# B and C casts behind bank copies, a spread decode, two tiles of the second layer by turns, and a shorter sign step

## The chip, the cores and the metric

The kernel runs on one core of a Trainium2 chip. The metric is the device time of one execution in microseconds (us). Times of a whole run stand beside a profiled execution, whose instructions the hardware profiler recorded. The engines are called as in the profile: PE (TensorE matmul; PEld its weight loads), DVE (VectorE), ACT (ScalarE), POOL (GpSimd) and SP (SyncE, which here only issues DMAs). An L and a number is a line of the kernel before.

## The reference

A chunked scan with decay, then two feed-forward layers on its output (batch 4, 8 heads, 768 positions, head size 32, state size 16). Cut to what is computed:

```python
for c in range(nc):                     # the reference goes by chunks of 32
    cum = np.cumsum(log_a[chunk]); L = np.exp(cum[i] - cum[j]) * causal
    y_intra = ((C @ B.T) * L) @ x       # per batch and head
    y_inter = (C @ state) * np.exp(cum)
    state = np.exp(sum(log_a)) * state + B.T @ (x * decay_from_j)
x = y.transpose(...).reshape(3072, 256)                       # tokens x (heads * head size)
h = max(max(x @ w1, x @ w2), x @ w3);  x = h @ w_out          # layer 1: 256 -> 768 -> 256
gate = 1 / (1 + exp(-(x @ w_gate)));  val = x @ w_val
return (gate * val) @ w_out2                                  # layer 2: 256 -> 1536 -> 256
```

The weights come in as 64-bit floats, seen as pairs of 32-bit words; the rest is float32.

## The kernel before

**Scan.** The kernel takes chunks of 96 positions, so there are 8 chunks and, with four of the 32 batch-head units at a time, 64 attention steps k = 8c + g. Step k does four matmuls s (B against C, L270 for the first 16 steps, L273 after), multiplies them with the decay (L285 on DVE, or L281 on ACT with L282 on POOL), and does four matmuls y (L291). For the steps from 16 on, s reads B and C as three bfloat16 parts each, stacked over partitions in `bi` and `cs`. `split_bc(c)` makes them for one chunk: it loads B and C into `bc` (L234); then three times over ACT casts what is left into `parts` (L239), SP sends `parts` to its places in `bi` and `cs` (L244, six, four and two DMAs for the three parts), and POOL takes the part away from `bc` (L248). `bc` and `parts` have one buffer, `bi` and `cs` two. The decay rows `dec` are loaded with L206 and scanned on DVE (L228). `prepare(k)` calls all of this ahead of its use; it adds `split_bc(c + 1)` to the pipe at step 8c.

**Layers.** Both layers go over six tiles of 512 tokens. A unit is a tile t and a block m of 128 hidden columns: layer 1 has 6 units a tile and three products (18 matmuls u, then 6 matmuls o into the accumulators), layer 2 has 12 units a tile and two products (12 u, 6 o). All of these are L338 to L340: each product is a sum of three, with operands split in a high and a low word. The three PSUM banks for u go round. A bank is emptied by `most` (layer 1: ACT copies the first bank, L383; DVE takes the maxima, L385 and L387) or `gated` (layer 2: ACT sigmoid, L392; DVE product, L394). Then ACT makes the high word (`hi`, L376), and POOL or DVE the low word (`lo`, L378). The matmuls o of a unit (`down`) come one unit later. The two accumulator banks `o0`, `o1` are copied out at the end of a tile (L357 to y1 for layer 1, L363 for layer 2). `split_y(t)` makes high and low words of layer 2's input (L369, L371).

**Decode.** Each weight piece of 128 x 512 (layer 1: 12 pieces `a`; layer 2: 24 pieces `b`, every other one 128 x 256) is loaded raw (L127) and turned into two float32 words: three ACT instructions (L136 the sign, into the upper half-words of the zeroed tiles `sg`; L138 the exponent, in place; L139 the low word, rounded), two on DVE (L142 shift and OR with the sign, L144 integer add), one on ACT (L148) and one on POOL (L150).

**Order.** The program is emitted as coroutines: `tick` moves each active one a stage on, and a slot (24 to a tile of layer 1) is one product or one `down`. `slot_end` starts attention steps so that a tile's input is there in time: for the first two tiles one at a time, from the third in pairs. `weights_tick` starts one decode a slot. The order on each engine is then laid by the framework's planner, which simulates the program with its own costs and may place an instruction well ahead of those that were emitted before it. Each engine then works through its list in that order. `tc.issue_after(x)` binds what is traced inside it to stand behind x on x's engine.

```python
act.copy(parts[:, p], r)                                   # L239
act.activation(out=sg...[..., 1], in_=f1.bitcast(F32), func=AF.Identity, scale=2.0 ** -112)   # L136
dve.scalar_tensor_tensor(out=t, in0=f1, scalar=3, in1=sg, op0=ALU.logical_shift_left, op1=ALU.bitwise_or)   # L142
```

Of the kernel before, what the change touches and what calls it, by code (L numbers as in the profile page):

```python
# [12 lines left out]
U32 = mybir.dt.uint32  # L13
AF = mybir.ActivationFunctionType
# [52 lines left out]
def scan_attention_then_ffn(ctx: ExitStack, tc: tile.TileContext, xh, ah, bch, pick, bn, w1, w2, w3,  # L67
# [48 lines left out]
    sgs = [stp.tile([128, DEC // 128, 128], I32, tag=f"sg{k}", bufs=1, name=f"sg{k}") for k in range(2)]  # L116
    blocks_done = []
    for sg in sgs:
        pool.memset(sg, 0)

# [9 lines left out]
    def decode(raw, wpool, blocks, name):  # L130
        nb = raw.shape[1]
        f1 = raw[..., 1]
        r = stp.tile([128, DEC // 128, 128], I32, tag="r", bufs=3, name=f"r_{name}")[:, 0:nb]
        sg = sgs[len(blocks_done) % len(sgs)][:, 0:nb]
        blocks_done.append(name)
        act.activation(out=sg.bitcast(F16).rearrange("p b (n t) -> p b n t", t=2)[..., 1], in_=f1.bitcast(F32),  # L136
                       func=AF.Identity, scale=2.0 ** -112)
        act.mul(f1.bitcast(F32), f1.bitcast(F32), 2.0 ** -112)  # L138
        act.mul(r, raw[..., 0].bitcast(U32), 2.0 ** -29)  # L139
        yield  # L140
        t = stp.tile([128, DEC // 128, 128], I32, tag="t", bufs=2, name=f"t_{name}")[:, 0:nb]
        dve.scalar_tensor_tensor(out=t, in0=f1, scalar=3, in1=sg, op0=ALU.logical_shift_left,  # L142
                                 op1=ALU.bitwise_or)
        dve.tensor_tensor(out=r, in0=t, in1=r, op=ALU.add)  # L144
# [3 lines left out]
        act.copy(w[:, 0], r.bitcast(F32))  # L148
# [4 lines left out]
    def weights_tick():  # L153
        if loaded:
            pipe.add(decode(*loaded.pop(0)))
# [75 lines left out]
    def split_bc(c):  # L231
# [6 lines left out]
        for p in range(3):  # L238
            act.copy(parts[:, p], r)  # L239
# [7 lines left out]
            if p < 2:  # L247
                pool.tensor_tensor(out=r, in0=r, in1=parts[:, p], op=ALU.subtract)  # L248
                yield

    steps = [(c, g) for c in range(NC) for g in range(NG)]
    done = [0]
    last = [None]
# [57 lines left out]
    def prepare(k):  # L311

        c, g = divmod(k, NG)
        if g == 0 and 0 < c < NC - 1:
            load_x(c + 1)
            pipe.add(split_bc(c + 1))
# [27 lines left out]
    def down(t, m, mn, w, hl, finish):  # L344
        if m == 0:
            acc[0] = [pso.tile([128, TT], F32, tag=f"o{d}", name=f"o{mn}_{t}_{d}")
                      for d in range(KD)]
        first = len(w) - KD
        for d in range(KD):
            three(acc[0][d], [m], mn, w, lambda k: first + d, lambda k: hl[0], lambda k: hl[1])  # L350
        if m == mn - 1:
            pipe.add(finish(t, acc[0]))
# [27 lines left out]
    def most(s, banks, hl):  # L380

        yield
        act.copy(s, banks[0])  # L383
# [3 lines left out]
        dve.tensor_tensor(out=s, in0=banks[2], in1=s, op=ALU.max)  # L387
        yield from hidden(s, hl, pool)

    def gated(s, banks, hl, eng):  # L390
        yield
        act.activation(out=s, in_=banks[0], func=AF.Sigmoid)  # L392
        yield
        dve.tensor_tensor(out=s, in0=banks[1], in1=s, op=ALU.mult)  # L394
# [169 lines left out]
```

## Time and profile before

| | |
|---|---|
| three timed runs | 606.14, 601.85, 602.65 us; median 602.65 us |
| the profiled execution: its time | 604.28 us |
| the profiled execution: span from first to last instruction | 602.5 us |
| mean granted TensorE clock over the span | 0.974 |
| PE busy | 563.0 us (93%) |
| DVE, ACT, POOL busy | 317.5, 260.0, 186.0 us |

Busy time is the time in which an engine has an instruction at work, added over the span. The clock is a share of full speed (2.4 GHz): 1.00 is full, 0.50 the lower level of 1.2 GHz. What an idle stretch is worth is read from the wait that ends it.

### The profile page before, as it was taken

How to read it: one execution, taken by the hardware profiler on the slowest of the kernel's cores; microseconds unless marked ns; L12 is line 12 of the kernel's file. 1: busy time of each engine (PE TensorE's matmuls, PEld its weight loads, DVE VectorE, ACT ScalarE, POOL GpSimd, SP SyncE). 2: the span in 40 equal slices, each digit the busy share in tenths (PEclk: the TensorE clock that was granted, in tenths of full speed). 3: DMA queues.
4: the chain of work that ended last, by engine and by line, in shares of the span. 5: the costliest groups of instructions: out<-in, count | busy, mean ns of one | idle time of the engine just before them, and what ended most of it. 6: DMA issues, size and time to landing. Idle time of an engine off the chain costs nothing.

```text
span 602.5 us, 8006 instructions
## 1 busy us (share of the span) xinstructions
PE 563.0 (93%) x2992; PEld 444.7 (74%) x2992; DVE 317.5 (53%) x467; ACT 260.0 (43%) x475; POOL 186.0 (31%) x207
## 2 busy tenths in 40 slices
PE   5778797997989999999999999999999999999997
PEld 4656575675767777777768888888888888888885
DVE  4899962644745755368987133344344334334332
ACT  5777653224233223279897243233233223223322
POOL 3668874335453424237668210000000000000000
PEclk9859998998999989999999999999999999999999
DMA  7998975373763900099000000000000000000000
GB/s 252 326 313 233 205 183 93 102 132 86 155 134 83 178 28 1 1 316 312 1 2 0 2 35 1 0 1 35 2 0 36 0 1 36 1 1 35 1 0 35
DMA packets 35367, 50.53 MB, mean 84 GB/s; under 512 B 3456, under 2 KB 24320, under 8 KB 35328
## 3 DMA queue, kind: packets, MB, share of 16 engines
q1 hardware_dynamic: 35328, 50.02, 32.0%
q8 instruction: 23, 0.38, 0.3%
q14 instruction: 16, 0.13, 0.1%
HBM read 38.51 MB, written 3.25 MB: 69 GB/s over the span
## 4 chain that ended last, share of the span: by engine, by line
PE 63%; DVE 9%; DMA 8%; ACT 5%; issue 4%; POOL 2%; SPq 1%; DVEq 0%; ACTq 0%; POOLq 0%
PE u L338 14%; PE u L339 14%; PE u L340 14%; PE o L339 7%; PE o L340 6%; PE o L338 6%; DMA cs<-parts 4%; DVE dec L228 2%; DMA dec<-ad 1%; DMA bc<-in_bch 1%; DVE t_b L142 1%; DVE s L387 1%; DVE s L385 1%; PE y L291 1%; POOL lo L378 1%
## 5 line engine op out<-in xcount | busy, mean ns | idle before, releaser
L376 ACT CAST hi<-s 128x512 fp32r<-128x512 f32 x108 | 67.1, 621 | 193.1 <-DVE s L394 153.8
L394 DVE TENSOR_TENSOR s<-u,s 128x512 f32<-128x512 f32 x72 | 49.7, 690 | 126.2 <-PE u L340 125.9
L338 PE MATMUL u<-xt_hi,w_b 128*128 128x512 f32 x288 | 112.4, 390 | 0.8 <-DVE s L385 0.6
L339 PE MATMUL u<-xt_lo,w_b 128*128 128x512 f32 x288 | 112.1, 389 | 0.0
L340 PE MATMUL u<-xt_hi,w_b 128*128 128x512 f32 x288 | 112.1, 389 | 0.0
L338 PE MATMUL u<-xt_hi,w_a 128*128 128x512 f32 x216 | 90.8, 420 | 10.4 <-ACT s L383 5.8
L339 PE MATMUL u<-xt_lo,w_a 128*128 128x512 f32 x216 | 87.2, 404 | 1.8 <-DVE xt_lo L302 1.8
L340 PE MATMUL u<-xt_hi,w_a 128*128 128x512 f32 x216 | 87.0, 403 | 0.0
L378 POOL TENSOR_TENSOR lo<-s,hi 128x512 fp32r<-128x512 f32 x48 | 66.4, 1384 | 64.1 <-ACT hi L376 63.0
L338 PEld LDWEIGHTS u<-xt_hi,w_b 128*128 128x128 f32 x288 | 54.1, 188 | 13.3 <-DVE s L385 1.1
L378 DVE TENSOR_TENSOR lo<-s,hi 128x512 fp32r<-128x512 f32 x60 | 41.5, 692 | 40.6 <-ACT hi L376 40.4
L340 PEld LDWEIGHTS u<-xt_hi,w_b 128*128 128x128 f32 x288 | 54.1, 188 | 11.3
L339 PEld LDWEIGHTS u<-xt_lo,w_b 128*128 128x128 f32 x288 | 54.1, 188 | 11.0
L338 PEld LDWEIGHTS u<-xt_hi,w_a 128*128 128x128 f32 x216 | 42.2, 195 | 25.1 <-ACT s L383 8.0
L228 DVE TENSOR_TENSOR_SCAN dec<-dec,delta 128x388 f32<-128x388 f32 x64 | 57.9, 944 | 3.2 <-DMA dec<-ad 3.0
L339 PE MATMUL o<-lo,w_b 128*128 128x512 f32 x144 | 56.1, 390 | 0.0
L340 PE MATMUL o<-hi,w_b 128*128 128x512 f32 x144 | 56.0, 389 | 0.0
L339 PEld LDWEIGHTS u<-xt_lo,w_a 128*128 128x128 f32 x216 | 42.1, 195 | 10.3 <-DVE xt_lo L302 2.3
L340 PEld LDWEIGHTS u<-xt_hi,w_a 128*128 128x128 f32 x216 | 42.0, 194 | 9.5
L392 ACT ACTIVATE s<-u 128x512 f32<-128x512 f32 x72 | 43.2, 600 | 10.8 <-PE u L340 9.8
L385 DVE TENSOR_TENSOR s<-u,s 128x512 f32<-128x512 f32 x36 | 24.6, 685 | 40.4 <-PE u L340 25.8
L338 PE MATMUL o<-hi,w_b 128*128 128x512 f32 x144 | 45.3, 390 | 0.5 <-ACT hi L376 0.5
(60 smaller groups left out, 761.6 us busy)
## 6 DMA issues: line engine op xcount, KB each, us to landing
dec<-ad SPq DMA_DIRECT2D x30, 388.0 KB, 5.6
raw_a<-in_w SPq DMA_DIRECT2D x18, 256.0 KB, 6.2
bi<-parts SPq DMA_DIRECT2D x36, 128.0 KB, 6.7
cs<-parts SPq DMA_DIRECT2D x36, 96.0 KB, 6.8
xs<-in_xh SPq DMA_DIRECT2D x6, 512.0 KB, 7.1
raw_b<-in_wg SPq DMA_DIRECT2D x12, 256.0 KB, 5.8
raw_b<-in_wv SPq DMA_DIRECT2D x12, 256.0 KB, 5.8
raw_b<-in_wo SPq DMA_DIRECT2D x12, 256.0 KB, 5.8
```

The source lines that it names most:

```text
L142: dve.scalar_tensor_tensor(out=t, in0=f1, scalar=3, in1=sg, op0=ALU.logical_shift_left, op1=ALU.bitwise_or)
L228: dve.tensor_tensor_scan(out=f, data0=f, data1=delta.rearrange("p u w -> p (u w)"), initial=0.0, op0=ALU.mult, op1=ALU.add)
L291: pe.matmul(y[32 * q:32 * q + 32, g % 4, 0:CH + N], xs[c][:, 4 * g + q, :], m[:, q, :], start=True, stop=True)
L338: pe.matmul(ps, wlo, a_hi(k), start=k == 0, stop=False)
L339: pe.matmul(ps, whi, a_lo(k), start=False, stop=False)
L340: pe.matmul(ps, whi, a_hi(k), start=False, stop=k == kn - 1)
L376: act.copy(hl[0], s)
L378: eng.tensor_tensor(out=hl[1], in0=s, in1=hl[0].bitcast(F32), op=ALU.subtract)
L385: dve.tensor_tensor(out=s, in0=banks[1], in1=s, op=ALU.max)
L387: dve.tensor_tensor(out=s, in0=banks[2], in1=s, op=ALU.max)
L392: act.activation(out=s, in_=banks[0], func=AF.Sigmoid)
L394: dve.tensor_tensor(out=s, in0=banks[1], in1=s, op=ALU.mult)
```

## The change

- `split_bc` isn't moved on by each tick, but by each `prepare(k)`: load at step 8c, then a part at each of the next three steps. For chunks 3 to 7 its casts stand behind the newest bank copy (L383 or L392) that has been emitted on ACT.
- The decode of layer 2's pieces stands, on ACT, behind that bank copy and, on DVE, behind the newest last reading of a bank (L387 or L394).
- From the last tile of layer 1 on, a decode is started in every third slot.
- Layer 2 does its first two tiles by turns, unit by unit, with a second pair of accumulator banks (`pso2`), which layer 1's last tile uses too. The low word of both tiles is made on POOL. `split_y(0)` and `split_y(1)` both come in layer 1's last tile.
- In the decode, the sign goes to the upper half-word of a tile `sr` and the rounded low word, as an unsigned 16-bit number, to the lower. DVE shifts (one source), then adds `sr` as one 32-bit word. The two `sg` tiles, their zeroing on POOL and the tile `t` go.

```diff
     def decode(raw, wpool, blocks, name):
         nb = raw.shape[1]
+        def behind(k):
+            return tc.issue_after(evict[k].ins) if name[0] == "b" else ExitStack()
         f1 = raw[..., 1]
         r = stp.tile([128, DEC // 128, 128], I32, tag="r", bufs=3, name=f"r_{name}")[:, 0:nb]
-        sg = sgs[len(blocks_done) % len(sgs)][:, 0:nb]
-        act.activation(out=sg.bitcast(F16).rearrange("p b (n t) -> p b n t", t=2)[..., 1], in_=f1.bitcast(F32),
-                       func=AF.Identity, scale=2.0 ** -112)
-        act.mul(f1.bitcast(F32), f1.bitcast(F32), 2.0 ** -112)
-        act.mul(r, raw[..., 0].bitcast(U32), 2.0 ** -29)
+        sr = stp.tile([128, DEC // 128, 128, 2], U16, tag="sr", bufs=3, name=f"sr_{name}")[:, 0:nb]
+        with behind(0):
+            act.mul(sr[..., 1].bitcast(F16), f1.bitcast(F32), 2.0 ** -112)
+            act.mul(f1.bitcast(F32), f1.bitcast(F32), 2.0 ** -112)
+            act.mul(sr[..., 0], raw[..., 0].bitcast(U32), 2.0 ** -29)
         yield
-        t = stp.tile([128, DEC // 128, 128], I32, tag="t", bufs=2, name=f"t_{name}")[:, 0:nb]
-        dve.scalar_tensor_tensor(out=t, in0=f1, scalar=3, in1=sg, op0=ALU.logical_shift_left,
-                                 op1=ALU.bitwise_or)
-        dve.tensor_tensor(out=r, in0=t, in1=r, op=ALU.add)
+        with behind(1):
+            dve.tensor_single_scalar(out=r, in_=f1, scalar=3, op=ALU.logical_shift_left)
+            dve.tensor_tensor(out=r, in0=r, in1=sr.rearrange("p b n t -> p b (n t)").bitcast(I32),
+                              op=ALU.add)
         yield
...
-        act.copy(w[:, 0], r.bitcast(F32))
+        with behind(0):
+            act.copy(w[:, 0], r.bitcast(F32))
...
-    def weights_tick():
-        if loaded:
+    def weights_tick(last=True):
+        if loaded and last:
             pipe.add(decode(*loaded.pop(0)))
...
         for p in range(3):
-            act.copy(parts[:, p], r)
+            with tc.issue_after(evict[0].ins) if c > 2 else ExitStack():
+                act.copy(parts[:, p], r)
...
-                yield
+            yield splits if p == 2 else None
...
             load_x(c + 1)
-            pipe.add(split_bc(c + 1))
+            splits.append(split_bc(c + 1))
+        if splits and next(splits[0], None) is splits:
+            splits.pop()
...
-            acc[0] = [pso.tile([128, TT], F32, tag=f"o{d}", name=f"o{mn}_{t}_{d}")
+            acc[t] = [psos[t % len(psos)].tile([128, TT], F32, tag=f"o{d}", name=f"o{mn}_{t}_{d}")
...
-        act.copy(s, banks[0])
+        evict[0] = act.copy(s, banks[0])
...
-        dve.tensor_tensor(out=s, in0=banks[2], in1=s, op=ALU.max)
+        evict[1] = dve.tensor_tensor(out=s, in0=banks[2], in1=s, op=ALU.max)
...
-        act.activation(out=s, in_=banks[0], func=AF.Sigmoid)
+        evict[0] = act.activation(out=s, in_=banks[0], func=AF.Sigmoid)
...
-        weights_tick()
+        weights_tick(t < NTT - 1 or s % 3 == 2)
...
+                psos.append(ctx.enter_context(tc.tile_pool(name="pso2", bufs=1, space=PSUM)))
...
-            if t == NTT - 1 and m == 3:
-                pipe.add(split_y(0))
+            if t == NTT - 1 and m in (2, 4):
+                pipe.add(split_y(m // 2 - 1))
...
-    for t in range(NTT):
-        for m in range(M2):
-            eng = pool if t == 0 else dve
+    order = [(t, m) for m in range(M2) for t in range(2)]
+    order += [(t, m) for t in range(2, NTT) for m in range(M2)]
+    for t, m in order:
+        eng = pool if t < 2 else dve
...
+            slot += 1
+            weights_tick(slot % 3 == 2)
```

## Rows read from the trace of the kernel before

**Rows 1.** The page, busy share in 40 slices of 15 us; PEclk is the granted clock.
```profile
PE   5778797997989999999999999999999999999997
...
PEclk9859998998999989999999999999999999999999
```

**Rows 2.** Sum 40 to 80 us; stages: start:end, length, PE PEld DVE ACT POOL busy, PEclk, DMA.
```profile
sum 40.00, PE 34.50 PEld 25.53 DVE 39.35 ACT 28.32 POOL 32.45; mean PE 17.25 PEld 12.77 DVE 19.67 ACT 14.16 POOL 16.22
...
100.25:107.00 6.75, 5.52 (x12) 3.71 (x12) 0.69 (x1) 3.20 (x5) 5.47 (x6) 0.50 0.04 5
...
141.20:144.55 3.35, 3.35 (x10) 2.57 (x9) 0.69 (x1) 1.81 (x3) 3.35 (x4) 0.50 0.11 27
...
140.99:185.85 44.86, 41.72 (x287) 31.21 (x287) 26.12 (x45) 16.31 (x30) 24.13 (x29) 0.96 0.54 119
...
212.90:216.20 3.30, 3.30 (x10) 2.56 (x9) 1.70 (x2) 0.81 (x2) 1.53 (x2) 0.50 0.39 120
...
256.00:310.00 54.00, 51.15 (x213) 38.81 (x212) 45.55 (x57) 47.50 (x99) 32.30 (x25) 1.00 0.53 175
310.00:580.00 270.00, 270.00 (x1192) 223.25 (x1191) 103.20 (x146) 95.71 (x170) 24.93 (x20) 1.00 0.03 10
```

**Rows 3.** Timeline of PE: start, length, instruction, [idle before <- what ended it].
```profile
100.27 1.28 PE L338 MATMUL o<-hi,w_a 128*128 128x512 f32 x2 [2.47 <-ACT hi L376]
102.76 0.79 PE L339 MATMUL o<-lo,w_a 128*128 128x512 f32 x1 [1.21 <-POOL lo L378]
...
140.77 0.50 PE L338 MATMUL u<-xt_hi,w_a 128*128 128x512 f32 x1 [3.81 <-ACT s L383]
...
175.54 0.50 PE L338 MATMUL u<-xt_hi,w_a 128*128 128x512 f32 x1 [1.45 <-ACT s L383]
...
211.68 0.33 PE L273 MATMUL s<-cs,bi 96*128 96x96 bf16 x4 [1.24 <-DVE s L385]
```

**Rows 4.** Timeline of ACT, the casts of B and C that waited longest.
```profile
98.28 0.94 ACT L239 CAST parts<-bc 128x896 bf16<-128x896 f32 x1 [9.06 <-DMA bc<-in_bch]
...
139.30 0.94 ACT L239 CAST parts<-bc 128x896 bf16<-128x896 f32 x1 [5.43 <-DMA cs<-parts]
...
174.07 0.94 ACT L239 CAST parts<-bc 128x896 bf16<-128x896 f32 x1 [5.85 <-DMA cs<-parts]
```

**Rows 5.** Waits of PE from 170 to 188 us: total, times, longest.
```profile
PE o L339 <- POOL lo L378: 1.2, 2, 0.8
```

**Rows 6.** Groups of DVE, ACT and POOL by shape: count, busy, mean ns, idle before.
```profile
L142 DVE SCALAR_TENSOR_TENSOR t_a<-raw_a,sg 128x512 int32<-128x512 int32 x12 | 11.4, 953 | 0.2
...
L224 DVE TENSOR_SCALAR dec<-dec 128x768 f32<-128x768 f32 x2 | 1.1, 560 | 4.4 <-DMA dec<-in_ah 4.4
L198 DVE TENSOR_SCALAR ac<-ac 128x192 f32<-128x192 f32 x1 | 0.3, 316 | 4.0 <-DMA ac<-in_ah 4.0
...
L136 ACT ACTIVATE sg<-raw_a 128x512 f16<-128x512 f32 x12 | 9.4, 786 | 3.1 <-DMA raw_a<-in_w 3.1
...
L139 ACT ACTIVATE r_a<-raw_a 128x512 int32<-128x512 uint32 x12 | 7.9, 657 | 0.0
...
L248 POOL TENSOR_TENSOR bc<-bc,parts 128x896 f32<-128x896 f32 x12 | 23.7, 1973 | 22.9 <-ACT parts L239 22.1 <-PE y L291 0.8
```

**Rows 7.** Line L142 from 34 to 82 us: ns min/median/max, first and last start.
```profile
L142 DVE SCALAR_TENSOR_TENSOR t_a<-raw_a,sg x10: 666/738/1644, 34.7 to 76.0; 128x512 int32<-128x512 int32 x10
```

**Rows 8.** Waits of SP's own queue over the span: total, times, longest.
```profile
SPq L244 <- PE s L273: 17.4, 4, 7.4
...
SPq L234 <- ACT parts L239: 11.5, 1, 11.5
```

**Rows 9.** Line L244: SP's time for one issue (ns min/median/max), and from issue to landing.
```profile
L244 SPq DMA_DIRECT2D cs<-parts x36: 547/597/1571, 26.7 to 200.6; - x36
...
DMA to landing us min/median/max: 3.0/6.7/9.4
```

**Rows 10.** The chain that ended last, from 188 to 213 us: start, length, what.
```profile
199.41 8.00 DMA dec<-ad
```

## What the change will do to the time

> **What bounds the kernel now.** I read the page first, then the stages, then PE's and ACT's timelines where PE stands still, last the DMA queue. The page shows PE at 9 in nearly every slice and its clock at 9 or full [rows 1]: this is a kernel bound by TensorE, and a gain must come from the places where PE waits or runs at the lower clock. The stages say where these are. From 310 to 580 us PE never pauses: 270.00 us busy of 270, 1192 matmuls, so 0.2265 us each [rows 2]. Nothing in the change makes a matmul shorter or removes one, so the steady part of layer 2 can't gain. What can is in three places.
>
> First, four pauses in layer 1's second to fourth tile. PE stood 2.47 us before 100.27 for `hi`, then 1.21 us for `lo`, 3.81 us before 140.77 and 1.45 us before 175.54 for the copy of a bank by ACT [rows 3]. ACT was not busy then. Its own timeline shows what it did: it sat 9.06, 5.43 and 5.85 us in front of a cast of B and C (L239), the first until the load of `bc` landed, the others until transfers out of `parts` landed [rows 4]. The bank copy that PE needed stood behind that cast and ran right after it. These casts weren't urgent. The one at 98.28 belongs to chunk 5, whose first step is k = 40, in the third tile; `split_bc(5)` is emitted at step 32, the first of that tile, which runs from 140.99 to 185.85 (the stretch between two copies of the accumulators [rows 2]). So the planner had brought it forward by some 40 us, to a place where in its own costs the load was there and in fact was not. Behind two of these pauses the clock fell: the granted clock is 0.50 (1.2 GHz) from 100.25 to 107.00 and from 141.20 to 144.55 [rows 2], each time after PE had stood still.
>
> Second, the stage from 40 to 80 us, where DVE is busy 39.35 of 40 us and PE 34.5 [rows 2]: the bound there is DVE, and a good part of what it does is the decode of layer 1's pieces.
>
> Third, the change of layers, 256 to 310 us: PE is idle 2.85 of 54 us while DVE and ACT have 45.55 and 47.50 us of work, most of it the decode of layer 2's pieces, put into one tile [rows 2].
>
> **The casts behind bank copies.** Removed are the three ACT pauses as PE feels them: 2.47 + 3.81 + 1.45 = 7.7 us. The cast of chunk 5 now can't run before the newest bank copy emitted at slot 50 of layer 1 (third tile), where before it ran at 98, about slot 24; `bc` has then been loaded for long, since its load isn't bound and only waits for the former chunk's third cast (slot 32). The wait for `lo`, 1.21 us, is the same delay handed on by POOL, so it goes too. Two more waits for `lo`, 1.2 us together from 170 to 188 us [rows 5], stand behind the same late chain and behind POOL's 1.97 us subtractions [rows 6], which remain; I count half, 0.6. The clock: PE was busy 5.52 + 3.35 = 8.87 us at the half level; at full clock the same matmuls take about half of it, so 4 us. Sum: 7.7 + 1.2 + 0.6 + 4 = 13.5 us; with all of the lo waits and a full half of 8.87 it would be 14.5. A third fall of the clock, at 212.90 [rows 2], comes from a late `dec` load (issued at 199.41, 8.00 us on its way [rows 10]), whose scan holds up DVE's copies and PE for 1.24 us [rows 3]; I leave it where it is.
>
> What the move queues up: at the new place a cast (0.94 us) stands directly behind a bank copy and ahead of the next `hi`, so each of the 15 bound casts may hold up the chain by a microsecond. The u banks are three, a product takes 6 x 0.2265 = 1.36 us, so such a delay is covered as long as it is under about one product. Two casts in a row with POOL's 1.97 us between them could reach 3 us on ACT. I charge 1 us for all.
>
> The price on the other side is lateness: from the third tile on steps go in pairs, and parts two and three of chunk 5 are both emitted at slot 53, while its first matmul s comes at slot 60. A slot there is 44.86 / 24 = 1.87 us [rows 2], so there are 13.1 us. Needed are two casts (0.94 each), POOL's 1.97 between them, two issues (0.597 each) and the landing, 6.7 us at the median and 9.4 at most [rows 9]: 11.7 to 14.4 us. It just fits or is late by 1.3 us. Chunks 6 and 7 have 13 slots, 24 us, and chunks 3 and 4 more than that. I charge 1 us. SP is helped rather than hurt: it now waits 17.4 us in front of L244 for the former readers of `bi` (matmuls s) [rows 8], because the casts came so early, and the `dec` loads behind it wait along.
>
> **The decode's sign and low word.** For each of the pieces DVE replaces a shift-and-OR with two sources by a shift with one. The trace has no one-source shift. The nearest rows are L224 and L198, one-source operations with the same kind of operands: 560 ns at 768 elements and 316 at 192 [rows 6], so 0.424 ns an element, and 452 ns at 512. The old instruction takes 666 ns at least and 953 in the mean, up to 1644 [rows 6, 7]; the 287 ns over the least are waits inside it. Ten of the twelve pieces `a` are in the DVE-bound stage [rows 7]. Bounds: nothing (a shift on integers as slow as the old form) to 10 x (0.953 - 0.452) = 5.0 us, if the waits go as well. I take the bare difference, 10 x 0.214 = 2.1 us, and count it in full since DVE has no slack there.
>
> The Trainium skill speaks to the waits inside: "SBUF — State Buffer", section "Who interferes with whom", says that a VectorE instruction in a two-port mode and any GpSimd instruction exclude each other for their whole length, and that one with two SBUF inputs does so against a GpSimd instruction that reads SBUF. By that the shorter shift would keep the waits of the old one, and hold up POOL in turn; the sum would be 2.1 us, not 5.0. The spread from 666 to 1644 ns [rows 7] fits it, and no row here shows the new form.
>
> ACT's two half-word writes are between 657 and 786 ns each (L139, L136 [rows 6]), so a piece changes by -0.13 to +0.13 us; ACT isn't the bound, and I count nothing. If its cover went, 10 pieces would be worth 1.3 us either way. The zeroing of `sg` on POOL runs before POOL has anything else: nothing.
>
> **The change of layers.** Seven decodes remain in layer 1's last tile instead of 23; the others follow one in three slots, which is one per unit. Each block of layer 2 needs two pieces and now lasts two units, so the lead of seven pieces is kept, some 28 us. All of this sits behind bank copies and beside units of 18 x 0.2265 = 4.08 us, in which DVE and ACT have, by the stage from 310 to 580, under 1.6 us of other work each [rows 2]. So PE's idle 2.85 us go, but for the sigmoid's first use, of which PE felt little: 2.7 us. POOL's low word for the second tile is longer than DVE's, but `down` comes a unit later. The second accumulator pair removes a dependency that cost PE nothing to speak of. If the decode came too late for a unit, the 2.7 us would be lost first.
>
> **Sum.** 13.5 + 2.1 + 2.7 - 1 - 1 = 16.3 us, from the profiled execution's own 604.28 us (span 602.5, 1.8 around it): 588.0. The median of the timed runs is 602.65, 1.6 lower, which would give 586.4. I say 587.
>
> **Rivals.** *Only half of the casts' gain*: the planner lays out the whole program anew, the freed chain meets what was next (a `dec` scan, POOL's subtraction), and half of 13.5 us stays. 595 us. For it: DVE's full stage and the `dec` load at 199.41 are there still, and a plan that was never run may have pauses of its own. Against: the pauses have one cause, and it is removed at its place.
>
> *The wait moves to the loads*: with the parts now sent in the tile in which the scan steps go in pairs, `dec` loads queue behind them on SP as at 199.41, once in each of tiles three to five. That case cost PE 1.24 us of waiting [rows 3] and half of 3.30 us at half clock [rows 2], 2.9 us.  Three or four more are 9 to 12 us: 596 to 599, and with none of the decode's gain up to 601. For it: the burst of parts from 190 us on held up just that load. Against: SP is freed of 17.4 us of waiting [rows 8].
>
> *Slower: the parts land after PE has come to s.* PE's list is in order, so a late `bi` or `cs` stops all matmuls behind it. It decides from a hold of SP's queue over 1.4 us for chunk 5 and over about 12 us for chunks 6 and 7; holds of 7.4 and 11.5 us are in the trace [rows 8]. One late chunk of 8 us, with the clock's fall behind it, costs 10 us; three of them 30: 617 us. Against: the long holds come from casts waiting and from early parts waiting for their buffers, which is just what goes.
>
> *The bind does nothing* (the planner had placed the casts behind those copies already): excluded by the cast of chunk 5 at 98.28, ahead of a third-tile copy by 40 us.
>
> **How the numbers follow.** A run-to-run difference under 1% is about what can't be told from no change, so faster means under 596.6 and slower over 608.7. My forecast (579 to 593) has 0.60, half the gain (593 to 597) 0.14, the loads 0.14 (most of it over 596.6), slower 0.09, and nothing at all, 600 to 606, 0.03. Low end: all waits, the decode's 5.0, no charges: 14.5 + 5 + 2.85 = 22.3 from 602.65, 580, and 2 us for what can't be seen: 578. High end: the loads, 601, and 1 more: 602. Faster: 0.60 + 0.11 + 0.03 = 0.74; same 0.17; slower 0.09.
>
> **What would show it.** In the new profile no wait of ACT in front of L239 over 3 us, PE's waits for `hi` and for the first copy of a bank under 1 us in all between 90 and 190 us, and no half clock near 100 and 141. The casts of chunk 5 run in the third tile. The shift at 0.43 to 0.50 us where POOL is idle. PE idle under 0.5 us in the last tile of layer 1 and the first units of layer 2, decodes going on until about 70 us into layer 2. I would be wrong if PE waited for `cs` or `bi` before a matmul s, if DVE's stage until 80 us stayed as long, or if new falls of the clock came with `dec` loads.

## The result, and the profile after

The changed kernel takes 585.24 us (median of 4 runs, 584.04 to 587.66), the kernel before, run beside it, 604.39 us (601.85 to 606.48): ratio 0.969, 95% interval 0.9634 to 0.9746. The profiled execution took 584.04 us with a span of 582.3 (before 602.5), 20.2 us less.

First the page of the changed kernel, PE's busy share and its clock, to be held against [rows 1]:

```profile
PE   4769879999999999999999999999999999999997
...
PEclk9859979999999999999999999999999999999999
```

From the seventh slice on, PE is at 9 and its clock with it, up to the last slice, in which the kernel ends. What is left lies in the first six slices. The stages say the same (start:end, length, then PE, PEld, DVE, ACT and POOL busy, clock, DMA), and answer to [rows 2]:

```profile
40.00:80.00 40.00, 33.49 (x217) 24.91 (x218) 35.02 (x50) 27.55 (x49) 29.18 (x28) 0.88 0.98 226
76.08:82.90 6.82, 4.62 (x10) 3.23 (x11) 5.71 (x11) 3.39 (x7) 4.55 (x4) 0.50 0.42 121
100.00:140.00 40.00, 40.00 (x265) 29.19 (x264) 23.43 (x39) 14.29 (x25) 18.54 (x23) 1.00 0.58 111
250.00:310.00 60.00, 60.00 (x267) 49.69 (x266) 30.41 (x50) 44.54 (x88) 32.09 (x26) 1.00 0.38 127
312.00:572.00 260.00, 260.00 (x1148) 215.35 (x1147) 92.96 (x141) 99.26 (x179) 35.19 (x29) 1.00 0.03 11
```

From 100 to 140 us, where PE had lost 2.47 and 3.81 us and its clock [rows 2, 3], it is busy 40.00 of 40. At the change of layers it is busy 60.00 of 60. The steady part is what it was (260.00 us for 1148 matmuls, 0.2265 each). From 40 to 80 us DVE has become free (35.02 where it had 39.35), but PE does less there than before, 33.49 us where it had 34.50, and its clock is at the half level from 76.08 to 82.90.

To see where the 20.2 us come from, I cut each profiled execution at PE's own milestones, since the same clock time means other work in another run: the first matmul of all (from it to the first matmul u is the start), the first matmul u of each tile of layer 1 (t0 to t5), of layer 2, and of its 25th unit (from there to the last matmul is the rest). This is worked out from the starts of the matmuls in the trace, in us; the last column is the idle time of PE from t1 to t3. The rows under the first two are the experiments of the next section.

```
                start    t0     t1     t2     t3     t4     t5   layer 2, 24 units   rest   idle t1-t3
before          27.47  52.49  46.94  48.62  43.62  37.79  35.63       99.67        199.79     12.3
after           28.16  58.24  38.20  40.97  40.02  37.63  32.64       96.56        199.43      0.7
casts_bound     31.12  53.35  38.16  40.97  39.82  37.63  35.49       99.67        199.43      0.3
casts_both      27.55  54.73  38.20  40.95  40.02  37.72  35.63       99.63        199.78      0.7
casts_steps     31.14  53.38  45.21  48.42  43.12  38.07  35.66       99.70        199.80     13.2
word_only       30.95  59.61  45.57  47.85  42.41  38.19  36.66       99.31        199.43     12.2
layer2_only     31.14  50.80  47.17  50.22  40.92  37.63  32.64       96.56        199.43     12.4
after_old_word  28.69  54.61  38.20  40.99  40.02  37.63  32.64       96.56        199.43      0.7
after_early     27.88  50.85  38.20  40.95  40.05  37.63  32.64       96.56        199.43      0.7
old_early       31.94  56.07  39.11  40.95  40.05  37.63  32.64       96.56        199.43      0.8
after_earlier   32.11  51.57  39.11  40.95  40.07  37.63  32.64       96.56        199.43      0.7
decode_free     31.80  57.42  38.20  40.99  40.07  37.63  35.34       99.86        199.43      0.7
decode_dense    28.95  57.59  38.20  40.99  40.07  37.63  32.86       99.52        199.44      0.7
word_early      30.65  51.77  46.56  47.65  43.93  37.63  36.45      100.71        199.41     11.8
```

Three entries make the result: t1 to t3 together 139.18 to 119.19, -20.0 us; t5 and the first units of layer 2 135.30 to 129.20, -6.1; t0 +5.75. The plan of the changed kernel does 30 matmuls o in t0 where before it did 26; four of them are 0.9 us that moved from t1, so the true figures are -19.1 and +4.85. The start differs by a few us between the executions, with PE's pace in it; the paragraph on the start, further down, takes it apart.

### The profile page after: what moved, and what is told of

Read it like the earlier page. It is cut to its first block, busy times and chain, and to the rows that moved or that the text cites. A ratio compares the mean times of both kernels' runs of the same rounds, so it can differ in the third digit from the quotient of the medians.

```text
span 582.3 us, 7999 instructions
## 1 busy us (share of the span) xinstructions
PE 554.8 (95%) x2992; PEld 444.1 (76%) x2992; DVE 290.0 (50%) x455; ACT 263.0 (45%) x475; POOL 196.5 (34%) x217
## 4 chain that ended last, share of the span: by engine, by line
PE 83%; DMA 8%; DVE 4%; ACT 2%; issue 1%; SPq 1%; DVEq 0%; ACTq 0%
PE u L344 19%; PE u L345 18%; PE u L346 18%; PE o L345 8%; PE o L344 8%; PE o L346 8%; PE y L295 2%; DMA raw_a<-in_w 2%; DMA raw_a<-in_wo 2%; DMA bx<-in_bn 1%; PE s L277 1%; DVE dec L229 1%; DMA bi<-parts 1%; DMA dec<-in_ah 1%; DVE xs L310 1%
## 5 line engine op out<-in xcount | busy, mean ns | idle before, releaser
L384 POOL TENSOR_TENSOR lo<-s,hi 128x512 fp32r<-128x512 f32 x60 | 82.3, 1372 | 108.9 <-ACT hi L382 108.9
L344 PE MATMUL u<-xt_hi,w_a 128*128 128x512 f32 x216 | 89.6, 415 | 6.7 <-ACT mt L285 4.4
L346 PE MATMUL u<-xt_hi,w_a 128*128 128x512 f32 x216 | 86.0, 398 | 0.0
L346 PEld LDWEIGHTS u<-xt_hi,w_b 128*128 128x128 f32 x288 | 54.1, 188 | 11.3
L344 PEld LDWEIGHTS u<-xt_hi,w_a 128*128 128x128 f32 x216 | 41.6, 192 | 19.3 <-ACT mt L285 5.0
L384 DVE TENSOR_TENSOR lo<-s,hi 128x512 fp32r<-128x512 f32 x48 | 33.2, 692 | 32.5 <-ACT hi L382 32.4
```

Source lines behind the costliest of these rows:

```text
L344: pe.matmul(ps, wlo, a_hi(k), start=k == 0, stop=False)
L346: pe.matmul(ps, whi, a_hi(k), start=False, stop=k == kn - 1)
L384: eng.tensor_tensor(out=hl[1], in0=s, in1=hl[0].bitcast(F32), op=ALU.subtract)
```

## The experiments

The theory after the result: the bind of the casts is worth some 19 us, the change of layers 6, and the decode word costs some 5, because the last raw piece comes too late for it. The rivals: the pacing of `split_bc` by steps does the work and not the bind; the word costs through its own slower instructions or through waits for POOL; or t0 is longer by an accident of the planner that no part owns. Each part was first run alone, then the suspected cause by itself.

**The casts: bind alone, pacing alone, both.** In the kernel before:

```diff
-            act.copy(parts[:, p], r)
+            with tc.issue_after(evict[0].ins) if c > 2 else ExitStack():     # casts_bound, casts_both
+                act.copy(parts[:, p], r)
...
-                yield
+            yield splits if p == 2 else None                                 # casts_steps, casts_both
...
-            pipe.add(split_bc(c + 1))
+            splits.append(split_bc(c + 1))                                   # casts_steps, casts_both
+        if splits and next(splits[0], None) is splits:
+            splits.pop()
```

Expected of the bind alone: 

> The kernel before, with only the casts of B and C for chunks 3 to 7 bound behind the newest bank copy on ACT; they still go on with each tick. My theory: the pauses of tiles two to four came from casts that the planner put too early, and the bind alone holds them back. In the changed kernel the second to fourth tile of layer 1 took 119.2 us against 139.2, so this kernel should be about 19 us faster than before (ratio 0.965 to 0.973), with no wait of ACT before a cast over 3 us after 85 us. Rival: the pacing by attention steps does it, and the bind adds little: then under 6 us (ratio over 0.99). Rival: the tile before is touched too (chunk 3's casts): then tile one differs from 52.5 us by more than 2.

Expected of both: 

> The kernel before, with the casts bound and split_bc moved on by the attention steps: the whole of this part. My theory: like the bind alone within 3 us, about 19 us faster than before (ratio 0.965 to 0.973). Rival: pacing matters as much as the bind: at least 5 us faster than the bind alone.

Expected of the pacing alone: 

> The kernel before, with split_bc moved on by the attention steps and no bind of its casts. Theory: the planner is as free as before to put a cast ahead of a bank copy, so most of the pauses stay: 0 to 6 us faster than before (ratio 0.99 to 1.00), ACT still waiting over 4 us in front of a cast at least once after 85 us. Rival: pacing alone does it, as the pair with the bind alone (0.9766) and both (0.9752) would allow: 12 us or more faster.

Measured: bind alone 587.68 us, ratio 0.9766 (0.9743 to 0.9789); both 586.27, 0.9752 (0.9726 to 0.9778); pacing alone 606.91, 1.007 (1.0048 to 1.0093). The first two gain less than the 0.965 to 0.973 expected, the third is a little slower than expected. The pacing alone leaves the waits where they were. The line L239 in its trace (count and ns; then what ACT waited for in front of it, in us and times), to be held against [rows 4]:

```profile
L239 ACT CAST parts<-bc x8: 930/938/939, 101.7 to 179.7; 128x896 bf16<-128x896 f32 x8
its engine sat idle before it (us, times) until:
  DMA cs<-parts: 11.4, 2
  DMA bc<-in_bch: 7.3, 1
  POOL bc L248: 4.1, 4
```

And PE's waits from 85 to 190 us in the same trace, then in that of the bind alone, where a single one is left (total, times, longest):

```profile
PE u L342 <- ACT s L387: 5.4, 2, 3.7
PE o L342 <- ACT hi L380: 3.3, 1, 3.3
PE o L343 <- POOL lo L382: 1.3, 2, 0.8
PE u L342 <- DVE s L391: 0.4, 1, 0.4
```

```profile
PE s L276 <- DVE s L388: 0.3, 1, 0.3
```

So the bind is the cause and the emission by steps isn't: each cast still goes into ACT's list where the planner wants it, unless it is bound. In the bind-alone kernel the coroutine still goes by ticks, and its casts of chunk 5 run at 131.46, 139.38 and 142.92 us; in the changed kernel they run at 133.34, 141.25 and 144.79.

**The decode word alone**, in the kernel before (sign and low word to `sr`, one-source shift, one add; no bind):

```diff
-        act.activation(out=sg.bitcast(F16).rearrange("p b (n t) -> p b n t", t=2)[..., 1], ...)
-        act.mul(r, raw[..., 0].bitcast(U32), 2.0 ** -29)
+        act.mul(sr[..., 1].bitcast(F16), f1.bitcast(F32), 2.0 ** -112)
+        act.mul(sr[..., 0], raw[..., 0].bitcast(U32), 2.0 ** -29)
...
-        dve.scalar_tensor_tensor(out=t, in0=f1, scalar=3, in1=sg, ...)
-        dve.tensor_tensor(out=r, in0=t, in1=r, op=ALU.add)
+        dve.tensor_single_scalar(out=r, in_=f1, scalar=3, op=ALU.logical_shift_left)
+        dve.tensor_tensor(out=r, in0=r, in1=sr...bitcast(I32), op=ALU.add)
```

Expected: 

> The kernel before, with only the decode's new word (sign and rounded low word in one added word, shift with one source). My prediction's step was a gain of 2.1 us in DVE's full stage. What the changed kernel showed: its first tile took 58.2 us against 52.5, with ACT waiting 4.9 us for the last raw piece and the clock falling after it. Theory now: the freed DVE time only moves the wait to the load of the last raw piece, so the total is 0 to 6 us longer than before (ratio 1.00 to 1.01). Rival: the decode is a gain of 2 us by itself (0.997) and the loss of the first tile comes from the moved casts of chunk 3. Rival: the shift loses to POOL what it saves, and the stage until 80 us stays as it was, within 1 us.

Measured: 611.64 us, ratio 1.0154 (1.0115 to 1.0194). It costs 9 us there, more than the 0 to 6 expected. In the profile t0 is 7.1 us longer, 6.2 without four matmuls o that this plan too moved into it; t1 to t3 are shorter and the start longer. The timelines of ACT, DVE and PE show how t0 came to it:

```profile
79.43 0.78 ACT L137 ACTIVATE sr_a<-raw_a 128x512 f16<-128x512 f32 x1 [6.76 <-DMA raw_a<-in_wo]
```

```profile
81.41 0.43 DVE L142 TENSOR_SCALAR r_a<-raw_a 128x512 int32<-128x512 int32 x1 [8.85 <-ACT raw_a L138]
81.75 0.68 DVE L389 TENSOR_TENSOR s<-u,s 128x512 f32<-128x512 f32 x1
```

```profile
82.49 0.79 PE L340 MATMUL u<-xt_hi,w_a 128*128 128x512 f32 x1 [7.53 <-DVE s L389]
```

ACT stood 6.76 us in front of the last raw piece. DVE's shift waited 8.85 us for ACT, and the maximum that empties a bank (L389) stood behind the shift in DVE's list; PE waited 7.53 us for that. None of these instructions is slow. But the load was later too, by SP's timelines, first of the kernel before, then of this one:

```profile
63.52 0.33 SPq L127 DMA_DIRECT2D raw_a<-in_wo  x1
```

```profile
70.90 0.47 SPq L123 DMA_DIRECT2D raw_a<-in_wo  x1
```

Its issue comes 7.4 us later, of which the longer start is 3.5. So this run alone doesn't separate a faster decode from a later load; the next runs do.

**The old word in the changed kernel, and raw loads moved ahead.** The loads of raw pieces hang on the loads of the decay rows `dec` (so many pieces behind the n-th of these):

```diff
-BEHIND = {4: 1, 5: 1, 6: 2, 7: 2, 8: 2, 9: 1, 10: 1, 11: 1, 12: 1}
+BEHIND = {4: 1, 5: 1, 6: 2, 7: 2, 8: 2, 9: 2, 10: 2}              # after_early, old_early, word_early
+BEHIND = {4: 1, 5: 2, 6: 2, 7: 2, 8: 2, 9: 2, 10: 1}              # after_earlier
```

Expected of the changed kernel with the old word: 

> The changed kernel with the old sign and low word of the decode. The new word alone cost 9 us in the kernel before (ratio 1.015). Theory: the new word is the part that works against the change, so that without it the kernel is 3 to 6 us faster than the changed one (585.2): 579 to 582. First tile of layer 1 52 to 55 us against 58.2. Rival, my prediction's step: the new word gains about 2 us here: 587.

Expected of the changed kernel with early loads: 

> The changed kernel with layer 1's last two raw pieces loaded behind the decay rows 9 and 10 instead of 11 and 12. Theory: what the new word costs is not its own time but that the last raw piece is asked for behind the parts' transfers (issued at 65.4, landed at 74.5) while its decode stands ahead of work that PE needs; asked for earlier, the 3.3 us pause and the clock's fall at 76 us go and the first tile takes 51 to 54 us: 579 to 582 in all. Rival: the new word's instructions are the cost (two half-word writes of 0.77 us on ACT, the shift that waits for POOL): then the first tile stays over 56 us.

Expected of the old word with early loads: 

> The changed kernel with the old word and the earlier loads. Theory: with no load to wait for, DVE's shorter shift shows: the new word with early loads is 1 to 3 us faster than this one. Rival: the two are the same within 1 us, and the word is worth nothing by itself; or this one is faster by over 2, and the new word is a cost of its own.

| in the changed kernel | loads as they were | early loads |
|---|---|---|
| old word | 580.07 us, 0.9623 (0.9593 to 0.9653) | 583.69 us, 0.9685 (0.9644 to 0.9725) |
| new word | 585.24 us, 0.969 (0.9634 to 0.9746) | 578.19 us, 0.9587 (0.9554 to 0.9621) |

With the loads as they were, the new word is some 4 us worse than the old one by the ratios; with early loads it is 6 better. The first difference by itself isn't settled, since its intervals overlap a little (0.9634 against 0.9653); the new word's own two cases don't overlap, and nor do the two with early loads. Each word has its better place for the loads among the two tried, and between these two versions lie 2 us, with overlapping intervals. The old word with late loads met its forecast (580 us, t0 54.6); the new word with early loads came out a little better than its own (578 us, t0 50.9), and its lead over the old word with early loads is larger than the 1 to 3 us expected.

The old word with late loads is the telling case: its last raw piece was issued at 65.18 us, as late as the new word's 65.40, but ACT came to it only at 74.87, and didn't wait. Until then it had waited for DVE. The same load is on time for the slower decode and late for the faster one. The stage from 40 to 80 us with the new word and early loads:

```profile
40.00:80.00 40.00, 37.86 (x252) 28.45 (x251) 38.73 (x59) 27.70 (x49) 31.69 (x33) 0.94 0.96 234
```

Its last raw piece was issued at 53.61 us instead of 65.40. DVE is full again (38.73 of 40) and PE does 37.86 us of work there instead of 33.49. From 34 to 100 us ACT has one wait for a raw piece left, 1.7 us, before the piece at 36.1, and none before the last; PE's longest wait there is 1.9 us, for `xt_lo`. This is the best version that was run.

**Still earlier loads.** Expected: 

> The changed kernel with the raw pieces of layer 1 loaded a further step earlier (two behind each of the decay rows 5 to 9, one behind 4 and 10). Loads one step earlier brought 578.2 us, first tile 50.9. Theory: the last piece is no longer what is late, so this is the same within 3 us: 576 to 581. Rival: the transfers of decay rows and parts are pushed back, and the first tile grows by over 2 us.

Measured: 583.34 us, 0.9671 (0.9638 to 0.9704), worse than the first early version and outside the 576 to 581 us expected; the rival's longer t0 isn't there either. In its profile t0 is 51.57 us with 26 matmuls o, no better, and the start is 32.11 us instead of 27.88; up to 46 us PE waits 4.0 us for `xt_hi`, where the first early version waits 1.3. Why the start is longer was not tried by itself.

**The word with early loads in the kernel before.** Expected: 

> The kernel before with the new word alone, and layer 1's last two raw pieces loaded behind the decay rows 9 and 10. The new word alone was 9 us slower than before, with the last piece landing at 79.3 us and PE waiting 7.5 us behind its decode. Theory: that landing is the whole of its cost, so with the earlier loads this is not slower than before: 595 to 604 (ratio 0.985 to 1.00), first tile under 54 us against 59.6, and no wait of PE over 4 us before 85 us. Rival: the word costs by itself in this kernel: over 607, first tile over 57 us.

Measured: 605.28 us, ratio 1.0051 (1.0011 to 1.0091), where the word alone had 1.0154. The t0 of 59.61 us is 51.77, 26 matmuls o in it, and the wait for the last piece is gone. So the lateness explains the larger part of the word's loss in the old kernel, 6 of 9 us by the ratios. It doesn't come out as fast as before, as it was expected to: the old casts' pauses stand there as they were, and t5 with the first units of layer 2 takes 137.16 us instead of 135.30, with the clock falling in t5 (0.953 in the mean). Why the plan came out worse there stays open.

**The second layer's part alone**, in the kernel before with its old word and its old casts (tiles by turns, second pair of accumulators, decode spread and bound):

```diff
+        with behind(0): ...      # on ACT, behind evict[0], for pieces b; on DVE behind(1)
...
-        weights_tick()
+        weights_tick(t < NTT - 1 or s % 3 == 2)
...
+    order = [(t, m) for m in range(M2) for t in range(2)]
+    order += [(t, m) for t in range(2, NTT) for m in range(M2)]
```

Expected: 

> The kernel before, with only the part at the change of layers: first two tiles of layer 2 by turns, a decode in every third slot from layer 1's last tile on, the decode of layer 2's pieces bound behind bank copies, the second pair of accumulator banks; old decode word, old casts. Theory: the last tile of layer 1 and the first 24 units of layer 2 lose all their pauses. They took 135.3 us before and 129.2 in the changed kernel, so 6 us faster (ratio 0.988 to 0.992). My prediction's step had 2.7 us (0.9955). Rival: the planner lays the earlier tiles anew and gives or takes more than 3 us there.

Measured: 596.42 us, ratio 0.993 (0.9902 to 0.9959). In its profile t5 and the first 24 units are 129.20 us, to a hundredth what the changed kernel has, so the 6.1 us are this part's own. The timed runs give 4 us, a little less than expected. The old pauses stay: PE is idle for 12.4 us from t1 to t3, as before, and these tiles take 138.31 us instead of 139.18.

**Of that part, the bind and the spread.** In the changed kernel, one with the decode not bound, one with a decode started in every slot:

```diff
-            return tc.issue_after(evict[k].ins) if name[0] == "b" else ExitStack()
+            return tc.issue_after(evict[k].ins) if False else ExitStack()      # decode_free
...
-            weights_tick(slot % 3 == 2)
+            weights_tick()                                                     # decode_dense
```

Expected without the bind: 

> The changed kernel without the bind on the decode of layer 2's pieces (they may stand ahead of bank copies again); spread and turns stay. Theory: with one decode in three slots ACT and DVE have so much room that the place doesn't matter: last tile of layer 1 32.6 us and first 24 units of layer 2 96.6 us, as in the changed kernel, within 0.5 each. Rival: the bind is what takes the pauses away: at least 2 us of the 6.1 come back.

Expected without the spread: 

> The changed kernel with a decode started in every slot, as before (no spread); turns and bind stay. Theory: the spread is the cause of the 6.1 us at the change of layers, so over 3 us come back, with waits of PE for ACT and DVE between 250 and 310 us. Rival: the bind suffices: under 1.5 us come back.

Measured: without the bind 592.84 us, ratio 0.9811 (0.9758 to 0.9865); t5 and the first 24 units take 135.20 us, so all 6 us are given back: the expectation was wrong, and its rival right. Without the spread 588.12, 0.9743 (0.9705 to 0.9781), and 132.38 us: 3.2 are given back, as expected. PE's waits from 235 to 350 us, first without the bind, then without the spread:

```profile
PE u L344 <- ACT s L398: 1.2, 1, 1.2
PE o L344 <- ACT hi L382: 1.1, 1, 1.1
PE u L344 <- ACT s L389: 0.7, 1, 0.7
PE o L345 <- POOL lo L384: 0.6, 1, 0.6
```

```profile
PE u L344 <- ACT s L398: 1.2, 1, 1.2
PE u L344 <- ACT s L389: 0.3, 1, 0.3
```

ACT's timeline in the trace without the spread, ahead of the wait for the sigmoid:

```profile
286.81 0.47 ACT L139 ACTIVATE sr_b<-raw_b 128x256 uint16<-128x256 uint32 x1
287.14 0.65 ACT L138 ACTIVATE raw_b<-raw_b 128x512 f32<-128x512 f32 x1
287.68 0.61 ACT L382 CAST hi<-s 128x512 fp32r<-128x512 f32 x1
288.31 1.28 ACT L398 ACT_TABLE_LOAD   x1
289.61 0.60 ACT L398 ACTIVATE s<-u 128x512 f32<-128x512 f32 x1
```

ACT comes from one piece of decode work to the next, and the load that the first sigmoid brings, 1.28 us, finds no slack any more. In the changed kernel the same load is covered. So both halves are needed: the bind without the spread gives 2.9 of the 6.1 us, the spread without the bind nothing. The turns of the two tiles and the second accumulators were in all of these runs; what they are worth by themselves wasn't tried.

## Why the prediction was right, and where it was not

The time came out near the forecast, and for the main part by its mechanism; but the terms of the sum were off in three places: the casts and the change of layers brought more than was counted, the word took where it was to give. That the sum ended within 2 us of the 587 forecast is luck, since these errors partly cancelled.

**The casts: mechanism right, term too small.** The sum had 13.5 us, less two charges of 1. The bind alone gives 14 us by its ratio (0.0234 of 601), and in its profile t1 to t3 lose 20.2 us, 19.3 without the four matmuls o that its plan too moved to t0. The start is 3.65 us longer there and takes part of that back, which is mostly not the bind's doing (see the start, below). The waits that were named are the ones that went. In the changed kernel, ACT's casts (count, busy, mean ns, then ACT's idle time in front of them), and PE's waits from 85 to 230 us:

```profile
L241 ACT CAST parts<-bc 128x896 bf16<-128x896 f32 x18 | 16.9, 938 | 4.4 <-DMA bc<-in_bch 2.3 <-POOL bc L250 2.1
```

```profile
PE u L344 <- DVE s L393: 0.4, 1, 0.4
PE s L277 <- DVE s L391: 0.3, 1, 0.3
```

ACT's waits before all 18 casts add up to 4.4 us (a single one was 9.06 before [rows 4]), and PE was idle for 0.7 us in 145 us. The casts of chunk 5 begin at 133.34, in the third tile (its first matmul u starts at 131.29), as forecast. Both charges were unfounded: a cast behind a bank copy cost PE nothing that shows, and no matmul s waited for `cs` or `bi`. The fall of the clock at 212.90, which the sum had left in place, went as well, with the 1.24 us of waiting before it. So the 19.1 us of t1 to t3 are made up thus: idle time fell from 12.3 to 0.7, 11.6 us where the sum had 9.5; PE was busy for 12.2 us at the half level (5.52, 3.35 and 3.30 [rows 2]) and is at full clock throughout now, some 6 us where the sum had 4; the 1.4 or so left over show neither as idle time nor as a lower clock, and are of the kind of the next point. About half of the 5.6 us that the term lacked is thus the third fall with its wait, which the prediction had priced at 2.9 us and left out.

**The change of layers: mechanism right, 2.7 us predicted, 6.1 measured.** The 2.85 us of idle time in [rows 2] were the wrong measure. A row of PE lasts 0.39 us, but matmuls start every 0.2265. In the kernel before, PE's timeline around one of these pauses:

```profile
288.53 0.39 PE L340 MATMUL o<-hi,w_a 128*128 128x512 f32 x1
289.41 0.50 PE L338 MATMUL u<-xt_hi,w_a 128*128 128x512 f32 x1 [0.50 <-DVE s L385]
289.75 0.40 PE L339 MATMUL u<-xt_lo,w_a 128*128 128x512 f32 x1
```

The idle time is printed as 0.50. From start to start it is 0.88, so 0.65 over 0.2265, and the next start is late by another 0.11 (0.34 instead of 0.23): 0.77 us lost for 0.50 shown. A stall shorter than 0.16 us shows no idle time at all. The right measure was at hand: t5 and the 24 units hold 570 matmuls of one kind, which need 570 x 0.2265 = 129.1 us; they took 135.3 before and 129.2 after. Counted over that stretch of before, 23 starts come late by 5.7 us in all, of which 8 show as idle time, 2.85 us. The same correction belongs to the pauses in t1 to t3, where it wasn't counted out. The rest of this point held: PE has no idle time there, and the shifts of layer 2's pieces go on until 351.5 us, 69 us into layer 2.

**The decode word: the step that failed.** It said -2.1 us, "in full since DVE has no slack there". The bare shift came out near the forecast; its saving in layer 1 was largely eaten by waits inside it. The shift and the low word by groups (count, busy, mean ns, idle before), to be held against [rows 6], and the shift's ten runs of layer 1 from 34 to 82 us (ns min/median/max), against [rows 7]:

```profile
L142 DVE TENSOR_SCALAR r_a<-raw_a 128x512 int32<-128x512 int32 x12 | 10.9, 912 | 4.9 <-ACT raw_a L138 4.5 <-issue 0.3
L142 DVE TENSOR_SCALAR r_b<-raw_b 128x512 int32<-128x512 int32 x12 | 5.1, 424 | 2.8 <-ACT raw_b L138 2.2 <-issue 0.6
L139 ACT ACTIVATE sr_a<-raw_a 128x512 uint16<-128x512 uint32 x12 | 9.2, 763 | 0.0
...
L142 DVE TENSOR_SCALAR r_a<-raw_a x10: 399/1013/1493, 37.5 to 77.1; 128x512 int32<-128x512 int32 x10
```

In layer 2 the shift takes 0.424 us at 512 elements (0.452 estimated, just under the 0.43 to 0.50 forecast). In layer 1 it still takes 0.912 in the mean, where the old one took 0.953. The least fell from 666 to 399 ns, but the median rose from 738 to 1013: added up from the trace, the ten take 9.78 us, where they took 9.73 before, so the waits inside grew by what the shift got shorter. The ten adds behind them (L144 before, L143 now) take 10.91 us instead of 12.07. So on these pieces DVE saves 1.1 us against the kernel before; against the changed kernel with the old word (10.89 and 11.79) it is 2.0, the size of the term, but half of it from the add. One of the waits beside POOL, DVE's timeline, then POOL's:

```profile
38.51 1.49 DVE L142 TENSOR_SCALAR r_a<-raw_a 128x512 int32<-128x512 int32 x1
```

```profile
37.98 1.73 POOL L151 TENSOR_TENSOR w_a<-r_a,w_a 128x512 fp32r<-128x512 f32 x1
```

POOL's instruction began first and ends at 39.71; the shift ends at 40.00. So it is with all eight shifts of layer 1 that last over 0.7 us: a POOL instruction was under way when they began, and they end 0.28 to 0.29 us after it. The Trainium skill's "SBUF — State Buffer", section "Who interferes with whom", has a VectorE instruction in a two-port mode wait for the whole GpSimd instruction that began before it; these eight agree with it, though no row shows which mode the shift is in.

The larger failure is at the end of the step. It asked what DVE has to do, not what is late next when DVE has less to do. In the changed kernel, all engines from 69 to 79 us:

```profile
69.24 0.48 ACT L285 COPY mt<-s 128x384 f32<-128x384 f32 x1
...
72.11 0.68 DVE L391 TENSOR_TENSOR s<-u,s 128x512 f32<-128x512 f32 x1
...
74.10 0.40 PE L295 MATMUL y<-mt,xs 128*32 128x112 f32 x8
...
74.59 0.78 ACT L137 ACTIVATE sr_a<-raw_a 128x512 f16<-128x512 f32 x1 [4.88 <-DMA raw_a<-in_wo]
...
76.92 0.46 ACT L304 CAST xt_hi<-y 128x384 fp32r<-128x384 f32 x1
77.10 0.97 DVE L142 TENSOR_SCALAR r_a<-raw_a 128x512 int32<-128x512 int32 x1 [4.31 <-ACT raw_a L138]
77.27 0.47 ACT L285 COPY mt<-s 128x384 f32<-128x384 f32 x1
...
77.80 0.79 PE L344 MATMUL u<-xt_hi,w_a 128*128 128x512 f32 x1 [3.30 <-ACT mt L285]
```

By 72.8 us DVE has nothing to do but wait, where before it was full until 80. The last raw piece, issued at 65.40, lands at 74.5. ACT stands 4.88 us in front of its first reading of it; the copy of `mt` for an attention step is behind that in ACT's list; PE waits 3.30 us for it and goes on at half clock until 82.90. The time DVE had saved came back as a wait for a load, on an engine whose list holds PE's work too. In the kernel before, the last piece was issued at 63.52 and the ten shifts ran until 76.0 [rows 7]: the decode was as late as the load, and the slack between them was what the new word used up. So the term was no gain of 2.1 us but a loss: 3.6 us in t0 and 4 by the ratios against the changed kernel with the old word, 9 in the kernel before, where the load came later as well. Only with the loads moved ahead is the new word the better one. The prediction named a sign close to it, "if DVE's stage until 80 us stayed as long", but neither the sum nor a rival had a price for it; the rival of the loads looked at `dec`, not at the raw pieces.

**The sum of the parts.** Alone the parts give -14 (casts), -4 (second layer) and +9 us (word) by their ratios, -9 together; the whole gives -19. The planner lays a new order for each program, and the word's loss and the old pauses of t1 and t2 come out differently beside each other. So parts run alone say which mechanism is at work, and not to the last us what it will be worth in the whole.

**The start.** Its 27 to 32 us differ mostly by PE's pace in that execution, not by the plan. Eight matmuls s of the scan in the kernel before, then in the bind alone:

```profile
15.14 1.13 PE L270 MATMUL s<-y 128*128 128x96 f32 x8
```

```profile
14.86 2.02 PE L273 MATMUL s<-y 128*128 128x96 f32 x8
```

They start every 0.112 us in the first and every 0.213 in the second, which is their pace in the kernel before from 26 us on, where its clock is given as 0.50. The clock printed from 10 to 20 us is 1.00 in both traces, so here the starts of the matmuls have to be read and not the clock. Of the 3.65 us by which the start of the bind alone is longer, 3.1 lie between the 25th and the 121st matmul (14.89 us for 11.77). Seven of the 14 profiles have 14.3 to 14.9 us there, the others 11.3 to 12.2; the changed kernel has 11.34, and the one without the decode's bind, which differs from it only in layer 2's pieces, 14.33. The start of the kernel with still earlier loads, 32.11 us, is another matter: this stretch takes 12.23 us there, and the waits above make it long.

**What stays open.** Why the old word with early loads (t0 56.07 us) is worse than the old word with late ones (54.61), why PE's pace at the start is the slow one in some executions, and what in the plan makes the rest of the start longer or shorter. Two profiles whose starts differ are better compared by the tiles behind it and by the timed runs.

## What to carry to other kernels

When an engine works in list order, an instruction that isn't urgent but waits for a transfer must be kept from standing in front of one that the bound engine needs; binding it behind a piece of that urgent work does this, and emitting it later need not. Before a saving on a full engine is counted, look up when the last input of that stage lands: if it is close behind, the load has to be moved ahead with it, or the saving turns into a wait. Price a pause of TensorE by the starts of its matmuls against their steady spacing, not by the idle time that the timeline prints.

## What the runs showed of the hardware

- A pause of PE can cost more than the idle time shown (0.77 us for 0.50 in the one taken apart above): the rows of single matmuls last 0.39 us and start every 0.2265, and the first after the pause was longer.
- ACT's write of half-words into every other place takes 0.763 us at 128 x 512 as an unsigned number and 0.788 as a 16-bit float, where the same reading written as whole words took 0.657 [rows 6]. The new word thus costs ACT 0.1 us a piece.
- A one-source shift on integers reading every other word takes 0.424 us at 512 elements, against 0.666 for the shorter runs of the two-source form [rows 7]. Beside POOL it lasts until 0.28 to 0.29 us after the end of the POOL instruction that began before it, in all eight cases over 0.7 us of the changed kernel.
- The same scan matmuls start every 0.112 us in some executions and every 0.213 in others, while the clock printed is 1.00 for both.
